# Attention with rotary positions and two feed-forward layers: loads of queries, keys, V and weights regrouped, one rotation on GpSimd alone, and the last products with V in two runs

## The chip, the cores and the metric

The kernel runs on one core of a Trainium2 chip. The metric is the device time of one execution in microseconds; less is better. TensorE (PE in the profile) multiplies matrices; its weight loads are shown as PEld. VectorE (DVE), ScalarE (ACT) and GpSimd (POOL) work on elements. SyncE (SP) issues the DMA transfers between HBM and on-chip memory. Each engine carries out its own instructions in order and waits for other engines by semaphores. TensorE's clock has two levels, 2.4 and 1.2 GHz; a granted clock of 1.00 is the upper one, 0.50 the lower.

## What is computed

The reference, cut to its core:

```python
def _attn_ref(q, k, v):            # (2, 8, 576, 64) each
    q_rot, k_rot = rotate(q), rotate(k)        # x1*cos - x2*sin, x1*sin + x2*cos
    scores = matmul(q_rot, k_rot^T) / sqrt(64)
    attn = exp(scores - max(scores))
    attn = attn / (sum(attn) + 1e-9)
    return matmul(attn, v)
def _moe_ref(x, w_in, w_out):      # 1152 tokens, 512 wide, 2048 hidden
    h = maximum(x @ w_in, 0)
    return h * h @ w_out
def _moe2_ref(x, w_a, w_b, w_out): # 512 wide, 1536 hidden
    return ((x @ w_a) * (x @ w_b)) @ w_out
```

Attention's output, heads side by side, is the input x of the first feed-forward layer, and that layer's output the input of the second.

## The kernel before

The sixteen heads are taken as eight pairs, p = 0 to 7; the two heads of a pair stand in the lower and upper 64 partitions. For each pair queries and keys are loaded into a tile X with planes for the value and for its half-swapped copy, each for queries and keys (`load_qk`, line 325); the load of a pair from 2 on is four transfers of 288 KB, one for each plane over all 128 partitions. `rotate` (line 344) multiplies by cosine and sine in place (line 356) and adds the two products (line 357), keys first, then queries. For pair 1 these four operations may go to VectorE or GpSimd; from pair 2 on GpSimd does them. X has two slots, so the load for pair p + 2 needs the rotation of pair p to be over.

A pair has five blocks c = 0 to 4, four of 128 query rows for each head and a fifth, half as much work, with the last 64 rows of both. For each block `scores` (line 383) puts eight matmuls (line 405, in the fifth block line 400) into one of two double banks `s0`, `s1`. VectorE takes them out with a negation that also finds the maximum (line 425), which frees the bank; ScalarE makes the exponentials and their sums (line 430); VectorE transposes them in blocks of 32 (line 446, `turned`). `times_v` (line 463) multiplies the transposed exponentials of the pair before with V, in five parts, into four banks AV[0] to AV[3], columns 0 to 192; one part is 64 or 48 small matmuls on TensorE (line 476). In TensorE's order, scores of the next block and a part of the products of the pair before alternate. Eight ScalarE copies (lines 307, 488 to 491) take the products out. `recip` (line 499) inverts the sums, with four small GpSimd operations (lines 509 to 512); `flip` (line 518) transposes them on TensorE, and `spread` (line 527) spreads them over partitions, into columns 192 to 480 of AV[0] and AV[1] for the last two pairs, where VectorE multiplies them with the products (line 542). Two more operations split the result into a high and a low part of x (lines 568 and 565).

`load_part` (line 452) runs after the blocks 0 to 3. It loads 32 partitions of V (288 KB, line 457) after a one-column ScalarE copy into the same place (line 455) that reads the sums of this block, so that the transfer can't start before the exponentials, and it hands in one of the four transfers of X of pair p + 2. That one is placed behind the copy in the plan, but does not touch what the copy writes.

Weights come as 64-bit words. `convert` (line 571) loads a raw tile of 512 KB (line 579, three slots), a ScalarE operation takes the upper halves (line 580), a clamp follows on GpSimd or VectorE (line 589), then a shift and a merge on VectorE (lines 583 and 586). The first `EARLY` = 4 weights are converted during attention: their clamp is on GpSimd, and the shift uses a score bank. The first three raw loads wait for a VectorE write into the slot (line 930) that follows the exponentials of the blocks named in `GATES`; conversions are spaced by `PACE` (line 906).

All operations are put into a `Plan` (line 69). TensorE's order is that in which they are written down. For the others the plan runs through time with a cost for each operation, gives every operation a due time worked back from TensorE, and takes the one that can start first, the earliest due among equals. A transfer costs 3.2 us for 1024 KB in the plan, plus 2.0 until others see it. The orders of TensorE, ScalarE, VectorE and GpSimd are then kept as planned (line 1001); SP is not in that list, and its order is made by the program builder from the data dependences.

After attention, `unit1` (line 690) makes a group of twelve matmuls of 384 columns for one block of the hidden layer, and `out1`, `super2` and `out2` do the rest of both layers, three matmuls for each product of numbers in two parts (lines 669 to 671, 876 to 878). The first list entries `steps` are unit1 for hidden blocks 0 to 3 with the first 384 tokens, which need only pairs 0 to 3; from the fifth entry on all pairs are needed. The loop at line 968 places what is left of the last two pairs between these entries at the places in `FILL`.

## Time and profile before

| | |
|---|---|
| median of 3 runs | 574.05 us (572.3 to 574.73) |
| the profiled execution | 578.77 us, of which its span, first to last instruction, is 577.0 us |
| TensorE busy | 550.0 us (95% of the span), 5318 matmuls |
| VectorE, GpSimd, ScalarE busy | 433.9, 305.3, 276.7 us |
| DMA | 58.45 MB, mean 101 GB/s |
| mean granted clock of TensorE | 0.967 |

The profile is one execution recorded on the chip. The table of stages gives for each stretch of time the busy time of each engine, with the number of instructions, the granted clock, the share of time that the DMA engines were busy, and their rate. The list of waits says which engine stood idle ahead of which line, and whose signal ended it ("issue" is idle time that ended without any signal that the profile shows). The chain of waits goes back in time from the last instruction, at each step to what released it. The timeline of an engine has start, duration, line, operation, output and input, count, and in brackets the idle time ahead of it with its releaser. The page's groups have busy time, mean nanoseconds of one, idle time ahead of them and its main releaser. The table of DMA issues has the number of transfers, their size, and the median time from issue to landing in us.

### The profile page before, as it was taken

Reading aid. Unit: us, or ns where it says so; the run is one execution under the profiler, and the core shown is the slowest. Engines: PE = TensorE matmul, PEld = TensorE weight load, DVE = VectorE, ACT = ScalarE, POOL = GpSimd, SP = SyncE. Lnnn points to the kernel's source line nnn. Section 1 sums busy time; section 2 is a strip of 40 time slices with the busy share of each in tenths; the row PEclk is TensorE's granted clock in tenths of the full one; section 3 lists DMA queues with packets and bytes.
Section 4 is the critical chain, followed back from the end, with each engine's and each line's share of the span. In section 5 each row is a group of like instructions: output and inputs, shape, how many; then the busy total and the mean of one; then the engine's idle time right before and its main releaser. Section 6 shows DMA issues by size and latency. Waiting matters only on the chain.

```text
span 577.0 us, 13042 instructions
## 1 busy us (share of the span) xinstructions
PE 550.0 (95%) x5318; PEld 491.5 (85%) x5318; DVE 433.9 (75%) x785; ACT 276.7 (48%) x652; POOL 305.3 (53%) x249
## 2 busy tenths in 40 slices
PE   7897689899889999999999999999999999999997
PEld 5565356666679999999999999999998999999986
DVE  5894697899639976944883759989787888886554
ACT  2453585667537756712730543565554544434210
POOL 2563798751327865812750537778676476765000
PEclk9798596899999999999999999999999999999999
DMA  7388377323204454411431201033331332310004
GB/s 239 112 224 209 121 232 191 91 74 84 65 3 154 157 202 145 147 36 37 149 108 37 73 1 37 2 110 132 123 101 51 108 110 74 110 38 1 1 0 164
DMA packets 18911, 58.45 MB, mean 101 GB/s; under 512 B 2313, under 2 KB 4489, under 8 KB 17828
## 3 DMA queue, kind: packets, MB, share of 16 engines
q1 hardware_dynamic: 18852, 57.63, 32.0%
q8 instruction: 41, 0.67, 0.5%
q14 instruction: 18, 0.15, 0.1%
HBM read 55.26 MB, written 2.36 MB: 100 GB/s over the span
## 4 chain that ended last, share of the span: by engine, by line
PE 83%; DVE 9%; DMA 3%; issue 2%; POOL 1%; ACT 1%; SPq 1%; DVEq 0%; ACTq 0%; POOLq 0%
PE m L669 13%; PE m L670 12%; PE m L671 12%; PE s L405 6%; PE av L476 6%; PE av L669 6%; PE av L670 6%; PE av L671 6%; PE m L876 3%; PE m L878 3%; PE m L877 3%; DMA raw_i<-in_w_in 2%; PE av L878 2%; PE av L877 2%; DMA X<-in_qk 2%
## 5 line engine op out<-in xcount | busy, mean ns | idle before, releaser
L565 POOL TENSOR_TENSOR g<-v,g 128x384 fp32r<-128x384 f32 (+1 forms) x41 | 48.9, 1195 | 43.0 <-ACT g L568 42.9
L430 ACT ACTIVATE PV<-PV,st 128x576 f32<-128x576 f32 x48 | 36.9, 769 | 40.5 <-DVE PV L425 40.3
L568 ACT CAST g<-v 128x384 fp32r<-128x384 f32 (+1 forms) x72 | 40.7, 566 | 25.9 <-DVE v L847 13.6
L425 DVE TENSOR_SCALAR_CACHE_REDUCE PV<-s 128x576 f32<-128x576 f32 x48 | 34.4, 753 | 11.9 <-PE s L405 11.6
L669 PE MATMUL m<-y,w_p 128*128 128x288 f32 x140 | 41.3, 295 | 0.7 <-DVE v L843 0.7
L670 PE MATMUL m<-y,w_p 128*128 128x288 f32 x140 | 41.2, 295 | 0.0
L671 PE MATMUL m<-y,w_p 128*128 128x288 f32 x140 | 41.1, 294 | 0.0
L405 PE MATMUL s<-cs_rot 64*128 64x288 f32 x128 | 32.0, 525 | 6.9 <-DVE PV L425 3.2
L476 PE MATMUL av<-PT_acc,PV 32*64 32x160 f32 (+1 forms) x1152 | 30.3, 326 | 7.2 <-issue 4.0
L356 POOL TENSOR_TENSOR X<-X,cs_rot 128x1152 f32<-128x1152 f32 x13 | 34.2, 2631 | 5.3 <-DMA X<-in_qk 5.3
L476 PEld LDWEIGHTS av<-PT_acc,PV 32*64 32x64 f32 x1152 | 23.5, 146 | 14.7 <-issue 9.2
L405 PEld LDWEIGHTS s<-cs_rot 64*128 64x128 f32 x128 | 17.6, 226 | 16.2 <-issue 6.8
L671 PE MATMUL m<-g,w_o 128*128 128x384 f32 (+1 forms) x92 | 29.3, 319 | 0.0
L670 PE MATMUL m<-g,w_o 128*128 128x384 f32 (+1 forms) x92 | 29.3, 318 | 0.0
L669 PE MATMUL m<-g,w_o 128*128 128x384 f32 (+1 forms) x92 | 29.3, 318 | 0.0
L708 DVE TENSOR_TENSOR v<-m,v 128x384 f32<-128x384 f32 x32 | 17.5, 551 | 15.3 <-ACT v L707 15.2
L589 POOL TENSOR_SCALAR cl_i<-cl_i 128x512 f32<-128x512 f32 x10 | 20.1, 2013 | 16.1 <-ACT cl_i L580 13.5
L717 DVE TENSOR_TENSOR oacc<-m,oacc 128x512 f32<-128x512 f32 (+1 forms) x29 | 19.4, 670 | 12.1 <-PE m L878 12.0
L669 PE MATMUL m<-x,w_i 128*128 128x384 f32 x84 | 28.5, 339 | 0.0
L717 DVE TENSOR_TENSOR yacc<-m,yacc 128x384 f32<-128x384 f32 (+1 forms) x28 | 14.2, 512 | 18.7 <-PE m L671 18.5
L671 PE MATMUL m<-x,w_i 128*128 128x384 f32 x84 | 28.1, 334 | 0.0
L670 PE MATMUL m<-x,w_i 128*128 128x384 f32 x84 | 28.1, 334 | 0.0
(246 smaller groups left out, 1958.2 us busy)
## 6 DMA issues: line engine op xcount, KB each, us to landing
PV<-in_vq SPq DMA_DIRECT2D x32, 288.0 KB, 3.4
raw_i<-in_w_in SPq DMA_DIRECT2D x16, 512.0 KB, 4.1
raw_o<-in_w_out SPq DMA_DIRECT2D x16, 512.0 KB, 3.7
X<-in_qk SPq DMA_DIRECT2D x26, 288.0 KB, 4.4
raw_a<-in_w_a SPq DMA_DIRECT2D x12, 512.0 KB, 3.7
raw_b<-in_w_b SPq DMA_DIRECT2D x12, 512.0 KB, 3.7
raw<-in_w_out SPq DMA_DIRECT2D x12, 512.0 KB, 3.6
out<-oacc SPq DMA_DIRECT2D x8, 256.0 KB, 2.0
```

The costliest lines, as they stand in the source:

```text
L356: m = pl.op(where, ("s", 2 * S), lambda e, qi=qi: e.tensor_tensor(out=x()[:, :, qi, :], in0=x()[:, :, qi, :], in1=cs, op=ALU.mult), [done[ ...
L405: pe.matmul(s[h]()[:, bk, 0:288], q0, k0[h][:, bk * 288:bk * 288 + 288], start=True, stop=True)
L425: m = pl.op("DVE", ("us", 0.7), lambda e, h=h, j=j: e.tensor_scalar(out=PP[pr.k][:, h, :].rearrange("p (b n) -> p b n", b=2), in0=s[h]()[: ...
L430: x = pl.op("ACT", ("us", 0.8), lambda e, h=h, j=j: e.activation(PP[pr.k][:, h, :], PP[pr.k][:, h, :], AF.Exp, bias=st()[:, 0, j:j + 1], s ...
L476: pe.matmul(AV[a]()[half(h), q], v[r, h, b], pt[r, k:k + 4 + both, 32 * b:32 * b + 32], start=(b == 0), stop=(b == KB - 1), skip_group_che ...
L565: e.tensor_tensor(out=out_, in0=a, in1=b, op=ALU.subtract)
L568: h = pl.op("ACT", ("s", n), lambda e: e.copy(hi_(), val()), after)
L669: pe.matmul(dst, wh, mh, start=first, stop=False, skip_group_check=open_)
L670: pe.matmul(dst, wh, ml, start=False, stop=False, skip_group_check=open_)
L671: pe.matmul(dst, wl, mh, start=False, stop=last, skip_group_check=open_)
L717: return pl.op("DVE", ("p", width), lambda e: e.tensor_tensor(out=acc(), in0=dst(), in1=acc(), op=ALU.add), [o] + b.prior, rel=[b])
L877: pe.matmul(b(), gt[:, 0, c], w[:, 1, d], start=False, stop=False)
```

## The change

Five things are edited.

- Queries and keys of pairs 2 to 7 are loaded in four parts of 32 partitions with all planes, after blocks 1 to 4 instead of one plane each after blocks 0 to 3. Behind blocks 3 and 4, where no part of V is loaded any more, a one-column ScalarE copy into the part of X comes first. `rotate` waits for all four parts.
- V's parts 0 and 1 are loaded after block 0, part 2 after block 1, part 3 after block 2 (`VAT`).
- The first three raw weight loads are gated by blocks (1,3), (2,0), (2,2) instead of (2,0), (2,2), (2,4), and in the plan every raw load ends `LATE` = 3.0 us later for those that wait for it.
- Pair 1 is rotated on GpSimd alone.
- Parts 0 and 1 of the last pair's products with V stay after the first entry of `steps`; parts 2 to 4 move behind the second one (`VFILL`). `flip` of the last pair, behind them, no longer waits in the plan for the products' banks.

```diff
+VAT = ((0, 1), (2,), (3,), (), ())
-GATES = ((2, 0), (2, 2), (2, 4))
+GATES = ((1, 3), (2, 0), (2, 2))
+VFILL = (0, 0, 1, 1, 1)
+LATE = 3.0
...
-            o.end, o.on, o.begin = s + took + self.LAG.get(e, 0.0), e, s
+            o.end, o.on, o.begin = s + took + o.late, e, s
...
-                for k, (qi, n) in enumerate(PLANES):
-                    LX[p, k] = lambda after, k=k, qi=qi, n=n: dma(288, lambda e: e.dma_start(out=b()[:, n, qi], in_=qk[p][:, n, qi]), after, acq=[] if k else [b])
+                for a in range(4):
+                    LX[p, a] = lambda after, a=a, r=slice(32 * a, 32 * a + 32): dma(288, lambda e: e.dma_start(out=b()[r], in_=qk[p][r]), after, acq=[] if a else [b])
...
-                where = FLEX if p == 1 else "POOL"
-                m = pl.op(where, ("s", 2 * S), lambda e, qi=qi: e.tensor_tensor(out=x()[:, :, qi, :], in0=x()[:, :, qi, :], in1=cs, op=ALU.mult), [done[qi, 0], done[qi, 1]])
+                where = "POOL"
+                m = pl.op(where, ("s", 2 * S), lambda e, qi=qi: e.tensor_tensor(out=x()[:, :, qi, :], in0=x()[:, :, qi, :], in1=cs, op=ALU.mult), list(done.values()))
...
-    def load_part(p, a):
-        r = slice(32 * a, 32 * a + 32)
-        ex, st = EXP[p, a][1][-1:], ST[p]
-        w = pl.op("ACT", ("us", 0.2), lambda e: e.copy(V4[r, p % 2, 0, 0, 0:1], st()[r, 1, 2 * a + 1:2 * a + 2]), ex + ([AVD[p - 2]] if p > 1 else []))
-        w.soon, w.anchor = 1.8, SDONE[p, a]
-        LV.setdefault(p, []).append(dma(288, lambda e: e.dma_start(out=V4[r, p % 2], in_=vq[p]), [w]))
-        if p + 2 < NPAIR:
-            if a == 0:
+    def load_part(p, c):
+        ex, st = EXP[p, c][1], ST[p]
+        for a in VAT[c]:
+            r = slice(32 * a, 32 * a + 32)
+            w = pl.op("ACT", ("us", 0.2), lambda e, r=r: e.copy(V4[r, p % 2, 0, 0, 0:1], st()[r, 1, 2 * c + 1:2 * c + 2]), ex[-1:] + ([AVD[p - 2]] if p > 1 else []))
+            w.soon, w.anchor = 1.8, SDONE[p, c]
+            LV.setdefault(p, []).append(dma(288, lambda e, r=r: e.dma_start(out=V4[r, p % 2], in_=vq[p]), [w]))
+        if c and p + 2 < NPAIR:
+            if c == 1:
                 load_qk_done[p + 2] = load_qk(p + 2)
-            load_qk_done[p + 2][PLANES[a]] = LX[p + 2, a]([w])
+            after = ex[-1:]
+            if not VAT[c]:
+                r = slice(32 * c - 32, 32 * c)
+                after = [pl.op("ACT", ("us", 0.2), lambda e: e.copy(XA[p + 2]()[r, 0, 0, 0:1], st()[r, 1, 2 * c:2 * c + 1]), ex[:1])]
+                after[0].soon, after[0].anchor = 1.8, SDONE[p, c]
+            load_qk_done[p + 2][c] = LX[p + 2, c - 1](after)
...
         o = pl.op("SP", ("dma", 512), lambda e: e.dma_start(out=raw_(), in_=src_of[key[0]][key[1]]), gate(), acq=[raw_])
+        o.late = LATE
...
-        if c < 4:
-            load_part(p, c)
+        load_part(p, c)
...
         if n == FILL[0]:
             last_spread(p - 1)
-            for k in range(len(PARTS)):
+        for k in range(len(PARTS)):
+            if n == VFILL[k]:
                 times_v(p, k)
         if n == FILL[1]:
-            flip(p, [Buf("av", None)], lambda: AV[2]().bitcast(BF16)[0:27, 896:1024])
+            flip(p, [], lambda: AV[2]().bitcast(BF16)[0:27, 896:1024])
```

## Rows read from the trace of the kernel before

**Rows 1.** Table of stages, cut where pairs 1 to 5 and unit1 begin.
```profile
27.34:41.10 13.76, 13.76 (x289) 9.30 (x288) 13.63 (x32) 8.54 (x24) 7.42 (x8) 1.00 0.72 189
41.10:68.18 27.08, 18.08 (x342) 11.73 (x339) 15.96 (x38) 11.65 (x37) 14.50 (x13) 0.76 0.71 181
68.18:86.00 17.82, 15.84 (x342) 10.76 (x339) 15.13 (x35) 11.75 (x36) 15.57 (x14) 0.88 0.71 220
86.00:106.15 20.15, 18.46 (x338) 12.32 (x338) 16.57 (x37) 12.71 (x38) 15.00 (x15) 0.75 0.69 180
106.15:120.67 14.52, 14.52 (x343) 10.13 (x338) 11.83 (x29) 9.93 (x31) 9.37 (x9) 0.88 0.26 75
...
168.76:577.00 408.24, 404.06 (x2505) 388.95 (x2502) 308.56 (x516) 186.93 (x375) 218.71 (x160) 1.00 0.25 85
```

**Rows 2.** List of waits of TensorE: waiting line, releaser, total us, times, longest.
```profile
PE s L400 <- DVE small L425: 6.6, 1, 6.6
...
PE s L405 <- DVE bits_i L586: 1.9, 2, 1.4
PE av L476 <- ACT PV L455: 1.4, 1, 1.4
```

**Rows 3.** Chain of waits, 46 to 60 us: start, duration, what.
```profile
46.09 1.42 POOL rot L357
...
47.53 0.33 SPq L330
...
49.80 10.05 DMA raw_i<-in_w_in
```

**Rows 4.** Timeline of ScalarE, the first weight's conversion.
```profile
59.88 0.66 ACT L580 ACTIVATE cl_i<-raw_i 128x512 f32<-128x512 f32 x1 [12.04 <-DMA raw_i<-in_w_in]
```

**Rows 5.** Timeline of VectorE in pair 0.
```profile
13.35 3.62 DVE L356 TENSOR_TENSOR X<-X,cs_rot 128x1152 f32<-128x1152 f32 x1
...
16.89 0.74 DVE L425 TENSOR_SCALAR_CACHE_REDUCE PV<-s 128x576 f32<-128x576 f32 x1
```

**Rows 6.** Timeline of TensorE, scores of pairs 0 and 1.
```profile
12.80 1.91 PE L405 MATMUL s<-cs_rot 64*128 64x288 f32 x8 [0.75 <-DVE PV L425]
...
17.79 2.87 PE L405 MATMUL s<-cs_rot 64*128 64x288 f32 x8 [2.21 <-DVE PV L425]
...
30.12 1.91 PE L405 MATMUL s<-rot 64*128 64x288 f32 x8
```

**Rows 7.** Timeline of GpSimd in pair 1, and the page's group of clamps.
```profile
31.38 2.64 POOL L356 TENSOR_TENSOR X<-X,cs_rot 128x1152 f32<-128x1152 f32 x1 [3.27 <-DMA X<-in_qk]
34.10 1.41 POOL L357 TENSOR_TENSOR cs_rot<-X 128x576 f32<-128x576 f32 x1
37.41 0.20 POOL L509 CAST part<-st 128x9 bf16<-128x9 f32 x1 [1.91 <-DVE st L506]
...
L589 POOL TENSOR_SCALAR cl_i<-cl_i 128x512 f32<-128x512 f32 x10 | 20.1, 2013 | 16.1 <-ACT cl_i L580 13.5
```

**Rows 8.** Timeline of ScalarE, exponentials of pair 0's last block.
```profile
28.00 0.77 ACT L430 ACTIVATE rot<-rot,st 128x576 f32<-128x576 f32 x1 [0.85 <-DVE rot L425]
```

**Rows 9.** DMA issues: X in 0:14, X in 27.3:41.1, V in 120.67:136.
```profile
X<-in_qk SPq DMA_DIRECT2D x4, 288.0 KB, 3.2
...
X<-in_qk SPq DMA_DIRECT2D x8, 288.0 KB, 5.3
...
PV<-in_vq SPq DMA_DIRECT2D x4, 288.0 KB, 3.2
```

**Rows 10.** Timeline of TensorE, the last pair's products with V.
```profile
155.11 3.02 PE L476 MATMUL av<-PT_acc,PV 32*64 32x160 f32 x138 [1.20 <-DVE xf L542]
159.43 2.42 PE L476 MATMUL av<-PT_acc,PV 32*64 32x160 f32 x128 [1.31 <-issue]
162.89 0.77 PE L476 MATMUL av<-PT_acc,PV 32*64 32x160 f32 x22 [1.03 <-issue]
```

**Rows 11.** Timeline of ScalarE, the copies that take these products out.
```profile
163.53 1.19 ACT L307 COPY xf<-av 128x128 f32<-128x128 f32 x8 [7.59 <-PE av L476]
```

More of the change, by code (lines that the diff above doesn't have):

```diff
@@ L62, in __init__ @@
         self.deps, self.acq, self.rel = list(deps), list(acq), list(rel)
-        self.end, self.soon, self.anchor, self.slack, self.urgent = None, None, None, 0.0, False
+        self.end, self.soon, self.anchor, self.slack, self.urgent, self.late = None, None, None, 0.0, False, 0.0
     def after(self, deps):
@@ L72 @@
     HOP = {"PE": 0.25, "SP": 2.0, "-": 0.0}
-    LAG = {}
     PORT = {"DVE": "POOL", "POOL": "DVE"}
@@ L322, in attention_moe_moe2_kernel @@
     XA, LX = {}, {}
-    PLANES = ((1, 0), (1, 1), (0, 0), (0, 1))
     def load_qk(p):
```

## The prediction

> **What bounds the kernel now.** I read the stage table first. Each pair of heads is cut where its first scores start, so that one line is one pair. From 168.76 us on, TensorE is busy for 404.06 of 408.24 us at full clock: nothing in this diff takes a matmul away there, so that part is fixed. Before it, the pairs take very unequal times for nearly equal work: 13.76, 27.08, 17.82, 20.15 and 14.52 us [rows 1]. With pair 5 as the measure, pair 2 has 12.6 us too many, pair 4 5.6 and pair 3 3.3, and the clock of these three is 0.75 to 0.88. Pair 0 fills the 27.34 us ahead of pair 1.
>
> Next the list of what TensorE waited for. The longest entry by far is one wait of 6.6 us for VectorE, in pair 2 [rows 2]. To see who made VectorE late, follow the chain of waits back through that place: GpSimd's last rotation of pair 3 ends at 47.51, only then does SP issue (47.53) the next of four loads of queries and keys, and the first weight tile goes out behind them at 49.80 and lands 10.05 us later [rows 3]. ScalarE meanwhile stands for 12.04 us at the conversion that wants this tile, with the exponentials behind it in its queue [rows 4]. SP is not among the engines whose order the plan writes out (line 1001), and counted from the start, four for a pair, these loads are those of pair 5, two pairs ahead.
>
> **The change, part by part.** The sum is made against the profiled execution, 578.77 us with a span of 577.0 (1.77 around it). It lies 4.7 us above the median of the three runs, 574.05.
>
> *GpSimd alone rotates pair 1.* In the kernel before, VectorE did one multiplication of 3.62 us at 13.35, and its next negation (`L425`), which frees a score bank, came at 16.89 [rows 5]. TensorE therefore idled for 2.21 us, and the following scores ran at half clock: 2.87 us for eight matmuls, where the same eight take 1.91 at full clock at 30.12 [rows 6]. Without that multiplication the first negation can begin when the second scores end, about 14.7 (they start at 12.80 and take 1.9). One negation of 0.7 us later there is a bank, so the third scores start at 15.4 instead of 17.79: 2.4 us. From there to pair 1 went 27.34 - 17.79 = 9.55 us; at full clock two steps of 2.78 (30.12 less pair 1's start at 27.34) and the short fifth block, for which I estimate 2.1 from these, give 7.7. Together -4.2 us; bounds -2.4 (the clock falls anyway) and -4.5. GpSimd must now do both products and sums, 2 x (2.64 + 1.41) = 8.1 us [rows 7], from about 13.2 to 21.3; pair 1 would start at 23.2, so 1.9 us hide it.
>
> *Rotation after the fourth part.* Until now the keys were rotated when their two planes had landed. Now the first multiplication waits for all four parts, and the fourth is tied by a ScalarE copy to the exponentials of the pair's last block. For pair 2 that block's exponential starts at 28.00 and takes 0.77 [rows 8]; the copy and the issue add about 0.5, the landing 3.2 to 5.3 us [rows 9], of which I take 4.2, near the middle, since V's and X's loads of one block still overlap; then 8.1 us on GpSimd, and the four small operations of line 509 on (1.1 us with their gaps) [rows 7], which fall into the middle and keep the flip in TensorE's queue waiting too. 28.8 + 0.5 + 4.2 + 8.1 + 1.1 = 42.7, where pair 2 started at 41.10: a new wait. All of it moves with pair 0's gain, so the price is +1.6 us, bounds 0.5 (landing 3.2) and +3 (landing 5.3, and the flip's delay on top). Behind it stand the scores and everything after them on TensorE. For pairs 3 to 7 the last exponential comes before or just at the next pair's start, so rotation ends some 13 us into a pair of 14.5 to 17: hidden, with 1.5 us to spare. Clamps of the early weights (two per pair in pairs 2 and 3) share GpSimd, so I add +0.5 for all five, bounds -0.5 and +5.
>
> *V sooner, first weights sooner, loads in parts.* V's last part is loaded after the third block, not the fourth; the 1.4 us wait on it (released through `L455`) [rows 2] goes. The first weight is gated on block (1,3) instead of (2,0), two blocks or about 5 us earlier, while its conversion stays paced by (2,0). Two of the four loads of a pair can't run ahead now, because a ScalarE copy writes into their tile first; the other two can, but only when the old rotation is done, which is now near the same pair's start. So the four loads of pair 5 no longer stand before the weight, and `LATE` puts the conversion later in ScalarE's order. Each conversion still costs VectorE 1.3 us by the plan's own figure (line 593) and may hold a score bank (1.9 us over two waits in pairs 2 to 4, [rows 2]). Pair 2 thus becomes like pair 3, which has two conversions: 17.82, less 1.3 for its share of half clock (0.12 x 17.82 = 2.1 us at most, part of which VectorE hides), 16.5. That is -10.6 us; bounds 14.5 (pair 5) and 24 (raw tile still half as late), so -12.5 and -3. Pair 3 itself: -1.3, bounds -3 and +1. Pair 4 ran at 0.75; I give it the middle between itself and pair 5, 17.3, which is -2.9, bounds -5 and 0. ScalarE's two extra copies of 0.2 us a pair lie in its idle time.
>
> A part now covers 32 partitions with rows four times as long. The rows show no penalty: undisturbed, V's loads, which have this very form, land in 3.2 us and the 128-partition planes of X also in 3.2 [rows 9]. The Trainium skill (SBUF — State Buffer, "Door 1: The DMA port swizzle") says otherwise: 32 partitions reach 8 of 16 ports, about 218 GB/s instead of 436. By that page a 288 KB part takes some 0.7 us longer on the wire, an estimate from its two rates; with three such parts queued the last one would be 2 us later, and the wait at pair 2 would be 3.6 instead of 1.6 us. The trace does not bear it out for single loads; for queued ones no row shows it.
>
> *Last pair's products in two runs.* Before, 288 products ran in one piece and TensorE stopped twice with nothing to wait for, 1.31 and 1.03 us, 128 products apart [rows 10]: it looks as if the stream of instructions ran dry. From one stop's end to the next is 162.89 - 159.43 = 3.5 us, the time that a stretch of 128 then takes to arrive. In the new order the 128 of the first two parts are followed by twelve large matmuls (2.3 us), then 160. The first stretch takes about 118 x 0.019 (2.42 / 128) plus ten of the twelve large ones, 1.9, so 4.1 us, and its stop goes; the second about 3.0 us, and keeps 0.5 of 1.03. That is -1.8. But the flip now follows the products at once. It writes into bank AV[2], which eight ScalarE copies of 1.19 us in all read [rows 11]. The same trace shows TensorE waiting 1.20 us for a VectorE operation that only reads other columns of its bank [rows 10], so I charge +1.0. Net -0.8, bounds -2.3 and +1.2. The flip has no cover: it stands in TensorE's queue ahead of unit1's third group, so a wait twice as long costs 1.0 more.
>
> *`LATE` on all weights* changes only the order of conversions after 168.76, where TensorE is 99% busy: 0, bounds -1 and +3.
>
> Sum: -4.2 + 1.6 + 0.5 - 10.6 - 1.3 - 2.9 - 0.8 = **-17.7 us**. Against the profiled execution that is 561.1; against the median 556.4. Part of the 4.7 us between these may be just the half-clock stretches that the change shortens, so I take a value between the two, nearer to the median's, **558 us**; its own range is 552 to 565.
>
> **The rivals.**
> *First weight still late.* SP's order is not in the plan, and two parts of each pair may still slip ahead and wait there for GpSimd. For: that is what happened at 41 to 47.5 [rows 3]. Against: two of four are now tied, and the gate is 5 us earlier. Then pair 2 keeps 7 to 9 us of its stall; 566 us. This is also the case in which the change doesn't do what it says.
> *GpSimd's rotation becomes the bound (slower).* Every pair from 2 on starts only when its rotation ends. A landing of 7.6 us instead of 4.2 under load (between X's 5.3 and the weight's 10.05 [rows 3, 9]), plus two clamps of 2.01 us ahead [rows 7], make 0.5 + 7.6 + 8.1 + 4.0 = 20.2 us per pair against 14.5: +5.7 in six pairs, 34 us, less the 17.7 gained, is 16 above the median: 590. It decides for slower from about 3.5 us per pair (six times that is 21, the gain and 0.5% of the time together). For: GpSimd was already busy for 15.57 of 17.82 us in pair 3 [rows 1]. Against: clamps have no early due time, and in pairs 5 to 7 there are none. At half that price, 17 us less 17.7, nothing would be left of the gain but a few us: 571 to 574.
> *The loads in parts land later.* Queued parts of 32 partitions may be slower than single ones; then the last part is late at pair 2, by up to the distance between the landings of 3.2 and 5.3 us [rows 9], 2 us: 560. For: in pairs 1 to 3 all loads queue. Against: V's loads in this form. By the port rule of that page of the Trainium skill this case would be the rule.
>
> **How the numbers follow.** Forecast 0.66; first weight late 0.12; the parts landing later 0.08; GpSimd at half price 0.06, at full price 0.08. The time is that of the likeliest. 551 to 568 takes in the forecast with the lower ends of its terms, the late weight and the late parts, and leaves out GpSimd's cases. About 0.5% is what a measurement of this kernel can tell from no change. Faster by more than that is everything up to 571: 0.66 + 0.12 + 0.08 and a sixth of the half-price case, 0.87; the rest of that case, 0.05, is no change, and the full price, 0.08, is slower.
>
> **What would show it.** In the changed kernel: the scores after 14.64 start near 15.4, with no multiplication at line 356 on VectorE; ScalarE's wait for the first weight falls from 12 us to under 2; TensorE's 6.6 us entry is gone and pair 2 takes under 18 us; a new wait of 0 to 3 us on GpSimd's rotation stands ahead of pair 2; the two stops in the last products shrink to one, with a wait on ScalarE's copies at the flip. From the fourth matmul group of unit1 on, the rest lasts 408 us as before. The prediction is wrong if the weight's load again leaves after loads of a later pair, or if rotation waits stand ahead of every pair.

## The result and the profile after

The changed kernel takes **565.52 us** (median of 4 runs, 563.62 to 566.12); the kernel before took 573.17 us in the runs beside it. The ratio is 0.9863, 95% interval 0.9821 to 0.9905: 7.65 us or 1.4% faster. The forecast was 558, its range 551 to 568: the direction and the range hold, the gain is about half of the 16 us that were forecast against the median. The profiled execution took 565.88 us with a span of 563.8, where before it was 578.77 and 577.0. Between the two spans the difference is 13.2 us, and why that is more than 7.65 is the first thing to be explained. The profiled execution of the kernel before counts as a slow one; e1 below profiles that kernel again.

The stage table of the changed kernel, cut as [rows 1] (pairs 1 to 5, then the rest from unit1's fourth group of matmuls on): the stretch, its length, busy time and instructions of TensorE, its weight loads, VectorE, ScalarE and GpSimd, then granted clock, DMA share and GB/s.

```profile
22.57:37.04 14.47, 14.20 (x289) 9.26 (x288) 13.42 (x32) 8.65 (x25) 8.76 (x8) 1.00 0.66 166
37.04:55.68 18.64, 15.13 (x341) 9.71 (x339) 15.83 (x37) 12.70 (x40) 12.07 (x11) 0.97 0.86 201
55.68:75.22 19.54, 17.97 (x340) 11.83 (x339) 14.77 (x35) 12.29 (x38) 15.06 (x13) 0.77 0.77 201
75.22:94.50 19.28, 17.19 (x338) 11.59 (x338) 17.64 (x34) 12.28 (x37) 14.57 (x13) 0.82 0.66 173
94.50:110.35 15.85, 14.73 (x344) 9.63 (x339) 13.76 (x32) 11.18 (x37) 10.26 (x10) 1.00 0.63 154
155.80:563.80 408.00, 403.90 (x2505) 388.90 (x2502) 311.96 (x517) 187.21 (x375) 213.32 (x159) 1.00 0.26 85
```

Pair 2 fell from 27.08 to 18.64 us, and pair 1 begins at 22.57 instead of 27.34. But pair 3 is longer than before (19.54 after 17.82), pair 4 hardly shorter (19.28 after 20.15), pair 5 longer (15.85 after 14.52), and pairs 3 and 4 run at granted clocks of 0.77 and 0.82. The last stretch is the 408 us that were expected.

What TensorE waited for, over the whole span (waiting line, releaser, total us, times, longest):

```profile
PE r L528 <- DVE bits_i L594: 2.5, 1, 2.5
PE s L406 <- DVE PV L426: 2.3, 6, 0.6
PE s L406 <- issue: 1.5, 2, 0.9
PE av L483 <- DVE xf L549: 1.2, 1, 1.2
PE s L406 <- DVE bits_i L594: 1.1, 2, 0.6
```

The entry of 6.6 us [rows 2] is gone, and so is the wait for V's last part. The longest left is 2.5 us, at a flip, for the bits of a weight.

Why the 6.6 us went is seen in SP's queue. First the kernel before, then the changed one, then ScalarE's conversion of the first weight in the changed one (a row of SP's timeline joins neighbours of a kind: start, time from the first issue to the end of the last, line, tile, count):

```profile
40.84 8.45 SPq L330 DMA_DIRECT2D X<-in_qk  x6
49.39 0.37 SPq L457 DMA_DIRECT2D PV<-in_vq  x1
49.80 0.42 SPq L579 DMA_DIRECT2D raw_i<-in_w_in  x1
50.33 14.64 SPq L457 DMA_DIRECT2D PV<-in_vq  x3
65.07 0.85 SPq L579 DMA_DIRECT2D raw_i<-in_w_in  x2
```

```profile
36.56 0.31 SPq L331 DMA_DIRECT2D X<-in_qk  x1
36.93 0.66 SPq L586 DMA_DIRECT2D raw_i<-in_w_in  x1
38.18 0.31 SPq L331 DMA_DIRECT2D X<-in_qk  x1
...
44.48 0.38 SPq L586 DMA_DIRECT2D raw_i<-in_w_in  x1
...
61.05 0.85 SPq L586 DMA_DIRECT2D raw_i<-in_w_in  x2
...
44.85 0.67 ACT L588 ACTIVATE cl_i<-raw_i 128x512 f32<-128x512 f32 x1
```

Before, six loads of X stood ahead of the first weight and held the queue for 8.45 us; after, the weight leaves at 36.93 with single loads of X around it, and ScalarE's conversion has no wait beside it, where it had 12.04 us [rows 4].

The tail, answering to [rows 10] (TensorE), with ScalarE's copies, answering to [rows 11]:

```profile
144.63 2.99 PE L483 MATMUL av<-PT_acc,PV 32*64 32x160 f32 x128 [1.20 <-DVE xf L549]
...
149.83 3.17 PE L483 MATMUL av<-PT_acc,PV 32*64 32x160 f32 x160
152.93 0.23 PE L528 MATMUL av<-small,part 128*27 128x128 bf16 x1
...
152.87 1.20 ACT L309 COPY xf<-av 128x128 f32<-128x128 f32 x8 [0.95 <-PE av L483]
```

Both stops within the products are gone, and the flip at 152.93 starts with no wait just after the first of ScalarE's copies of the products began at 152.87.

### The profile page after: what moved, and what is told of

Read it like the earlier page. It is cut to its first block, busy times and chain, and to the rows that moved or that the text cites. A ratio compares the mean times of both kernels' runs of the same rounds, so it can differ in the third digit from the quotient of the medians.

```text
span 563.8 us, 13068 instructions
## 1 busy us (share of the span) xinstructions
PE 547.1 (97%) x5318; PEld 488.6 (87%) x5318; DVE 435.6 (77%) x785; ACT 280.2 (50%) x664; POOL 302.2 (54%) x249
## 4 chain that ended last, share of the span: by engine, by line
PE 82%; DVE 9%; ACT 3%; DMA 2%; issue 2%; POOL 1%; SPq 0%; DVEq 0%; ACTq 0%; POOLq 0%
PE m L677 13%; PE m L679 13%; PE m L678 13%; PE av L677 6%; PE av L678 6%; PE av L679 6%; PE av L483 6%; PE s L406 4%; PE m L886 3%; PE m L885 3%; PE m L884 3%; DMA X<-in_qk 2%; DVE PV L426 1%; PE av L886 1%; PE av L885 1%
## 5 line engine op out<-in xcount | busy, mean ns | idle before, releaser
L572 POOL TENSOR_TENSOR g<-v,g 128x384 fp32r<-128x384 f32 (+1 forms) x39 | 47.4, 1217 | 47.0 <-ACT g L575 46.7
L575 ACT CAST g<-v 128x384 fp32r<-128x384 f32 (+1 forms) x72 | 40.8, 567 | 30.8 <-DVE v L855 16.2
L678 PE MATMUL m<-y,w_p 128*128 128x288 f32 x152 | 44.8, 295 | 0.0
L679 PE MATMUL m<-y,w_p 128*128 128x288 f32 x152 | 44.7, 294 | 0.0
L677 PE MATMUL m<-y,w_p 128*128 128x288 f32 x152 | 44.7, 294 | 0.0
L357 POOL TENSOR_TENSOR X<-X,cs_rot 128x1152 f32<-128x1152 f32 x14 | 36.6, 2634 | 11.4 <-DMA X<-in_qk 8.5
L406 PE MATMUL s<-cs_rot 64*128 64x288 f32 x128 | 28.4, 455 | 4.7 <-DVE PV L426 2.0
L406 PE MATMUL s<-rot 64*128 64x288 f32 x128 | 29.6, 473 | 1.3 <-issue 0.9
L483 PE MATMUL av<-PT_acc,PV 32*64 32x160 f32 (+1 forms) x1152 | 29.0, 315 | 1.6 <-DVE xf L549 1.2
L725 DVE TENSOR_TENSOR oacc<-m,oacc 128x512 f32<-128x512 f32 (+1 forms) x32 | 21.6, 679 | 10.9 <-PE m L886 10.8
L678 PEld LDWEIGHTS m<-y,w_p 128*128 128x128 f32 x152 | 28.5, 188 | 1.0
L677 PEld LDWEIGHTS m<-y,w_p 128*128 128x128 f32 x152 | 28.5, 188 | 0.9
L716 DVE TENSOR_TENSOR v<-m,v 128x384 f32<-128x384 f32 x32 | 17.6, 552 | 15.0 <-ACT v L715 15.0
L572 POOL TENSOR_TENSOR w_i<-bits_i,w_i 128x512 fp32r<-128x512 f32 x10 | 13.0, 1302 | 29.4 <-ACT w_i L575 29.3
L572 DVE TENSOR_TENSOR g<-v,g 128x384 fp32r<-128x384 f32 (+1 forms) x33 | 24.2, 732 | 5.8 <-ACT g L575 5.6
L679 PEld LDWEIGHTS m<-y,w_p 128*128 128x128 f32 x152 | 28.6, 188 | 0.0
```

The source lines that it names most:

```text
L357: m = pl.op(where, ("s", 2 * S), lambda e, qi=qi: e.tensor_tensor(out=x()[:, :, qi, :], in0=x()[:, :, qi, :], in1=cs, op=ALU.mult), list(d ...
L406: pe.matmul(s[h]()[:, bk, 0:288], q0, k0[h][:, bk * 288:bk * 288 + 288], start=True, stop=True)
L483: pe.matmul(AV[a]()[half(h), q], v[r, h, b], pt[r, k:k + 4 + both, 32 * b:32 * b + 32], start=(b == 0), stop=(b == KB - 1), skip_group_che ...
L572: e.tensor_tensor(out=out_, in0=a, in1=b, op=ALU.subtract)
L575: h = pl.op("ACT", ("s", n), lambda e: e.copy(hi_(), val()), after)
L677: pe.matmul(dst, wh, mh, start=first, stop=False, skip_group_check=open_)
```

## The experiments

The table gives, for each kernel, its median and its ratio to the kernel before (with interval) and, from its profiled execution, the start of pair 1, the lengths of pairs 1 to 5, and the time from pair 7's start to the end. The kernel before had medians of 571.9 to 573.6 us in the runs beside e1 to e12.

| kernel | median us | ratio (95%) | pair 1 at | pairs 1 / 2 / 3 / 4 / 5 | pair 7 to end |
|---|---|---|---|---|---|
| before | 574.05 | – | 27.34 | 13.76 / 27.08 / 17.82 / 20.15 / 14.52 | 441.1 |
| changed | 565.52 | 0.9863 (0.9821–0.9905) | 22.57 | 14.47 / 18.64 / 19.54 / 19.28 / 15.85 | 438.7 |
| e1_before_again | 572.83 | 1.0021 (0.9988–1.0054) | 22.97 | 13.78 / 28.56 / 17.25 / 19.20 / 15.12 | 441.2 |
| e2_pool1_alone | 572.43 | 1.0003 (0.9979–1.0028) | 23.65 | 14.46 / 23.38 / 17.72 / 19.62 / 15.03 | 441.0 |
| e3_gates_undone | 569.33 | 0.9955 (0.9939–0.9971) | 23.52 | 14.46 / 20.34 / 21.08 / 16.73 / 17.64 | 440.2 |
| e4_clamp_vector | 570.26 | 0.9963 (0.9930–0.9997) | 23.83 | 14.47 / 18.85 / 20.43 / 18.89 / 17.98 | 440.2 |
| e5_split_undone | 565.84 | 0.9871 (0.9819–0.9923) | 23.35 | 14.46 / 18.30 / 19.98 / 17.27 / 15.84 | 441.5 |
| e6_loads_undone | 571.16 | 0.9962 (0.9937–0.9987) | 23.12 | 14.46 / 19.86 / 16.17 / 23.84 / 14.47 | 441.5 |
| e7_shift_in_sbuf | 568.74 | 0.9928 (0.9903–0.9953) | 23.14 | 14.46 / 18.16 / 16.58 / 21.91 / 16.24 | 440.2 |
| e8_no_small_add | 566.54 | 0.9882 (0.9833–0.9931) | 23.80 | 14.46 / 17.81 / 17.70 / 20.21 / 17.98 | 440.3 |
| e9_bridge | 566.99 | 0.9910 (0.9876–0.9944) | 23.75 | 14.46 / 20.14 / 17.30 / 19.15 / 14.65 | 440.2 |
| e10_v_undone | 564.56 | 0.9857 (0.9804–0.9910) | 24.10 | 14.46 / 17.15 / 20.01 / 18.21 / 15.48 | 438.8 |
| e11_late0 | 566.42 | 0.9882 (0.9822–0.9942) | 23.07 | 14.46 / 16.15 / 19.83 / 18.37 / 18.65 | 439.8 |
| e12_two_alone | 563.37 | 0.9835 (0.9790–0.9881) | 23.18 | 15.42 / 15.43 / 21.03 / 15.58 / 15.26 | 440.9 |

### Was the profiled execution of before typical?

The kernel before, unchanged, profiled once more; and the kernel before with one line of the change.

> The kernel before, unchanged, profiled once more. The first profiled execution took 578.77 us, 5.6 more than the median 573.17. Theory: that execution was an unlucky one, and the extra time lies in the stretches at half clock of pairs 2 to 4 (65.05 us in all); this profile then shows a span of about 571 with some 60 us for the three pairs, and the wait of ScalarE for the first weight still over 8 us. Rival: the profile itself adds the time; then the span is 576 to 577 again, with the three pairs at 65.

```
-                where = FLEX if p == 1 else "POOL"
+                where = "POOL"
```

> The kernel before with pair 1 rotated on GpSimd alone, nothing else. Theory: pair 1 starts at about 22.6 instead of 27.3 us, as in the changed kernel, and all that follows moves with it, since the load that the first weight waited behind hangs on the same rotations: 568.5 to 569.5 (-4). Rival: the wait in pair 2 is set by loads that don't move and eats it: 572 to 573.

e2 took the rival's 572.4 us. Neither theory foresaw what e1 showed: pair 1 began at 22.97 with no line changed, while pairs 2 to 4 took the same 65.0 us as in the first profile. The profiled execution of e1 took 575.89 us, still 3.1 above its median, so it isn't a typical one either. That of e2, whose edit turned out to be worth nothing, took 571.86, within 0.6 us of its median; its pair 2 took 23.38 us, with a wait of 5.73 us for the first weight where the two others had 12.04 and 13.53. The rows are those of the one multiplication on VectorE. First GpSimd in the first profile of before (VectorE's row beside it is in [rows 5]), then VectorE and GpSimd in e1:

```profile
13.12 2.63 POOL L356 TENSOR_TENSOR X<-X,cs_rot 128x1152 f32<-128x1152 f32 x1 [1.20 <-DMA X<-in_qk]
```

```profile
13.22 1.35 DVE L356 TENSOR_TENSOR X<-X,cs_rot 128x1152 f32<-128x1152 f32 x1
...
13.47 3.59 POOL L356 TENSOR_TENSOR X<-X,cs_rot 128x1152 f32<-128x1152 f32 x1 [1.68 <-DMA X<-in_qk]
```

In the first profile GpSimd began 0.23 us ahead of VectorE, and VectorE's operation took 3.62 us; in e1 VectorE began 0.25 us ahead and took 1.35, and GpSimd's took 3.59 instead of 2.63. So the 3.62 us on which the first term of the sum rested hung on which of two operations started a quarter of a microsecond ahead of the other. Taken alone, in e2, the line is worth nothing: 1.0003, with pair 1 longer by 0.7 us.

### The parts undone, one at a time

```
-GATES = ((1, 3), (2, 0), (2, 2))
+GATES = ((2, 0), (2, 2), (2, 4))
```

> The changed kernel with the first three raw weights gated as before, by blocks (2,0), (2,2), (2,4). Theory: what had made the first weight late were the loads of a later pair in front of it, and the tied loads in parts cure that alone; the load then leaves some 5 us later and lands about when the conversion wants it: 565 to 567, ScalarE waits under 3 us. Rival: the earlier gate is the cure; then ScalarE waits 4 us or more for the weight and the time is 568 to 571.

```
-                for a in range(4):
-                    LX[p, a] = lambda after, a=a, r=slice(32 * a, 32 * a + 32): dma(288, lambda e: e.dma_start(out=b()[r], in_=qk[p][r]), after, acq=[] if a else [b])
+                for k, (qi, n) in enumerate(PLANES):
+                    LX[p, k] = lambda after, k=k, qi=qi, n=n: dma(288, lambda e: e.dma_start(out=b()[:, n, qi], in_=qk[p][:, n, qi]), after, acq=[] if k else [b])
```

> The changed kernel with one part undone: X loaded by planes (keys first, two planes, then queries) instead of by 32 partitions, V's parts one after each of the first four score groups as before, and the rotation of keys waits for its own two planes alone. Gates, split, pair 1 and the later due time of the weights stay as changed. Theory: the rotation that waits for all four parts is what holds GpSimd's clamp back in pair 2 (a wait of 2.83 us for X, with the clamp behind it at 49.59 us); with planes the rotation of keys starts earlier, the clamp and the shift behind it come earlier, and the time falls to 562 to 564.5 us beside 565.5. Rival: V's earlier parts and the loads by partitions are worth as much as they cost or more, and planes bring back longer waits for V or for queries: 566.5 to 569.5 us.

Both cost: 3.8 us against the changed kernel for the gates (569.33, the rival's time, but without the wait of ScalarE that the rival named) and 5.6 us for the loads (571.16, beyond even the rival's). SP's queue and ScalarE in e3, then in e6:

```profile
43.13 0.41 SPq L586 DMA_DIRECT2D raw_i<-in_w_in  x1
...
51.73 0.66 ACT L588 ACTIVATE cl_i<-raw_i 128x512 f32<-128x512 f32 x1
```

```profile
37.48 0.42 SPq L581 DMA_DIRECT2D raw_i<-in_w_in  x1
37.95 7.58 SPq L332 DMA_DIRECT2D X<-in_qk  x4
...
62.58 1.75 SPq L332 DMA_DIRECT2D X<-in_qk  x4
...
64.90 0.85 SPq L581 DMA_DIRECT2D raw_i<-in_w_in  x2
...
73.34 0.66 ACT L583 ACTIVATE cl_i<-raw_i 128x512 f32<-128x512 f32 x1 [3.77 <-DMA raw_i<-in_w_in]
```

(The diff of the loads is cut to the transfers of X; the blocks behind which they leave, V's place and the rotation's waits are as before there too.) With the old gates the first weight leaves at 43.13 instead of 36.93 and its conversion comes at 51.73 instead of 44.85; pair 3 then takes 21.08 us. In this trace TensorE also stops for 3.40 us, with no signal that ends it, near the end of pair 2 (until 57.59); whether that belongs to the gates is not shown. With the old loads the first weight leaves in time (37.48), but four planes of X hold the queue for 7.58 us right behind it, and later four more stand ahead of the third weight. It leaves at 64.90 (61.05 in the changed kernel), ScalarE waits 3.77 us for it, and its conversion comes at 73.34, where pair 4 begins; that pair takes 23.84 us. So the two parts do different things for the same weights: the gates let the first one leave early, and the loads in parts keep the later ones from standing behind loads of X that are not wanted yet. Each without the other leaves a gain of 0.4%, the two together 1.4% or more (e12 below).

The other parts, undone:

```
-VFILL = (0, 0, 1, 1, 1)
+VFILL = (0, 0, 0, 0, 0)
...
-            flip(p, [], lambda: AV[2]().bitcast(BF16)[0:27, 896:1024])
+            flip(p, [Buf("av", None)], lambda: AV[2]().bitcast(BF16)[0:27, 896:1024])
```

> The changed kernel with one part undone: the last pair's five groups of products with V are issued in one run again, behind the first unit, and the transpose of the sums' parts acquires the banks again. In the changed kernel the stretch from the first product of the MoE's first unit to the end of the last group took 15.14 us, where it took 17.62 us in the kernel before. Theory: the whole 2.5 us belongs to the split, so this kernel takes 567.5 to 568.5 us beside the changed kernel's 565.5, and the two stops of TensorE in the fourth and fifth groups are back, between 1 and 2 us each. Rival: only the 0.8 us of the prediction belong to the split, the rest being the earlier arrival of what the last pair needs; then 566 to 566.8 us.

```
-VAT = ((0, 1), (2,), (3,), (), ())
+VAT = ((0,), (1,), (2,), (3,), ())
```

> The changed kernel with V's parts loaded after the first four score groups, one each, as before; X stays in parts of 32 partitions after groups two to five, and all else as changed. With planes for X and the old place of V together the time was 571.16 us beside the changed kernel's 565.5, with waits of TensorE for V (1.7 us) and for products of the pair before the last (2.8 us). Theory: V's late last part, which lies behind X's plane in the queue, makes that loss: 568.5 to 571 us here too. Rival: the form and order of X's loads makes it, V's place does not matter: 565 to 567 us.

```
-LATE = 3.0
+LATE = 0.0
```

> The changed kernel with the estimate of the weights' landing 3 us shorter, as before. The order that the planner writes changes: ScalarE converts the first early weight ahead of the exponentials of its group instead of behind the first of them, and the same for the third and fourth. Theory: the weights land by then (ScalarE did not wait for the first at 44.85 us), so the place is worth less than 1 us: 565 to 567 us. Rival: the conversion moves ahead of the landing, ScalarE waits for the raw weight in pair 2 with exponentials queued behind it, and pair 2 takes over 20 us: 568 to 571 us.

None of the three moves the time by what these runs can tell from nothing (+0.3, -1.0 and +0.9 us against 565.52, each with intervals of about 3 us to either side). So it was not V's place that cost 5.6 us in e6, but the form and order of X's loads. With `LATE` at 0 the first conversion does not wait either (the second waits 1.15 us; pair 2 took 16.15 us), against its rival. Without the split the stops within the last products come back: one of 1.24 us in e5, two of 0.89 and 1.31 in e12 below. The split is small, and the last column of the table gives its size best: from pair 7's start to the end the nine traces with the split take 438.7 to 441.5 us, 440.0 in the mean, and the five without it 440.9 to 441.5, 441.1 in the mean. That is 1.1 us, between groups that overlap and that differ in other parts too, nearer to the 0.8 of the forecast than to the 2.5 that the first pair of profiles seemed to show.

### Where the rest of the gain went

Four theories about the stops that are left in pairs 2 to 5. In the changed kernel the longest begins as follows (GpSimd, VectorE, TensorE):

```profile
44.40 5.23 POOL L357 TENSOR_TENSOR X<-X,cs_rot 128x1152 f32<-128x1152 f32 x2 [2.83 <-DMA X<-in_qk]
49.59 1.92 POOL L597 TENSOR_SCALAR cl_i<-cl_i 128x512 f32<-128x512 f32 x1
...
51.55 0.69 DVE L591 TENSOR_SCALAR up_i<-cl_i 128x512 int32<-128x512 int32 x1 [1.31 <-POOL cl_i L597]
52.28 0.69 DVE L594 SCALAR_TENSOR_TENSOR bits_i<-raw_i,up_i 128x512 int32<-128x512 int32 x1
...
53.11 0.22 PE L528 MATMUL r<-small,part 128*27 128x128 bf16 x1 [2.52 <-DVE bits_i L594]
```

ScalarE has converted the weight by 45.5, but the clamp stands on GpSimd behind the rotation of pair 3, which waits 2.83 us for X's fourth part. VectorE waits for the clamp, the flip waits for a score bank that the shift's result holds, and from 54.5 us on the granted clock is at its lower level (0.50) for 10.2 us.

The clamps on VectorE:

```
-            o = pl.op("POOL", ("clamp", DM), lambda e: clamp(e, cl), [o])
-            o = pl.op("DVE", ("us", 1.3), lambda e: (shift(e, cl), merge(e)), [o], acq=[up] + bits.acq, rel=[raw_, cl, up])
+            o = pl.op("DVE", ("us", 2.0), lambda e: (clamp(e, up), shift(e, up), merge(e)), [o], acq=[up] + bits.acq, rel=[raw_, cl, up])
```

> The changed kernel with the clamps of the first four weights on VectorE, into the score bank that the shift uses anyway, instead of on GpSimd. Theory: in the changed kernel the first clamp stood behind pair 3's rotation on GpSimd (49.59, though its input was ready at 45.5), VectorE stood 1.31 us for it, TensorE 2.52 us, and the clock then fell to half for 10.24 us; with the clamp off GpSimd that wait and this stretch go: 560 to 562. Rival: it is the shift's hold of a score bank that stops TensorE, and this makes it 0.7 us longer: 565 to 568.

The time rose by 4.7 us, and the waits for bits of a weight grew from 3.6 us (2.5 and 1.1 in the list above) to 6.5:

```profile
PE s L406 <- DVE bits_i L594: 4.7, 3, 2.1
...
PE r L528 <- DVE bits_i L594: 1.8, 1, 1.8
```

So moving the clamp to VectorE costs more than it gives. What its place on GpSimd costs by itself is not shown, since the edit also makes VectorE hold the bank longer. The bank itself is tried with this edit, after which shift and merge hold none (with `up` taken out of the list of what is acquired and released):

```
-        up = Buf(STAGS, {t: lazy(lambda t=t: sps.tile([P, 2, 512], F32, tag=t, name=f"up_{name}")[:, 0]) for t in STAGS}) if early else bank_t()
+        up = cl if early else bank_t()
```

> The changed kernel in which the four early conversions shift in place in the clamped tile in SBUF, and merge from there, so that they hold no bank of the scores. Theory: TensorE's longest remaining waits (2.5 and 1.1 us for bits of a weight) and the half clock behind them come from the score bank that shift and merge hold while the shift waits for GpSimd's clamp; without the bank pair 2 to pair 5 lose 3 to 5 us together (73.3 us now, 68 to 70 then), 560.5 to 562.5 us, and no wait of TensorE for bits of a weight is left in the attention. Rival: the shift, now with both ends in SBUF, is stretched by GpSimd's products (from 0.69 to 2 us or more), VectorE's negations wait behind it, and the waits only change their name: 565 to 569 us.

The waits for bits are gone, as meant, and the time is 3.2 us worse. The price is on VectorE, where shift and merge now read and write SBUF (two of the four weights):

```profile
51.55 1.59 DVE L591 TENSOR_SCALAR cl_i<-cl_i 128x512 int32<-128x512 int32 x1
53.17 1.77 DVE L594 SCALAR_TENSOR_TENSOR bits_i<-raw_i,cl_i 128x512 int32<-128x512 int32 x1
...
81.53 0.89 DVE L591 TENSOR_SCALAR cl_i<-cl_i 128x512 int32<-128x512 int32 x1
82.46 3.00 DVE L594 SCALAR_TENSOR_TENSOR bits_i<-raw_i,cl_i 128x512 int32<-128x512 int32 x1
```

0.69 us became up to 3.00 beside GpSimd's products, and TensorE's longest wait for VectorE's negations (line 426) rose from 0.6 to 2.2 us: the rival's mechanism. So e7 doesn't show what the bank costs by itself. Then the small addition, which in the changed kernel took this long:

```profile
81.11 2.55 DVE L512 TENSOR_SCALAR st<-st 128x9 f32<-128x9 f32 x1
...
81.00 5.21 POOL L357 TENSOR_TENSOR X<-X,cs_rot 128x1152 f32<-128x1152 f32 x2 [3.47 <-DMA X<-in_qk]
```

```
-            e.tensor_scalar_add(st()[:, 1, :], st()[:, 1, :], 1e-9)
+            pass
```

> The changed kernel without the addition of 1e-9 to the sums of exponentials (128 by 9 elements, once in each pair), which took 2.55 us beside GpSimd's product in pair 3, 0.13 to 0.17 us elsewhere. This addition is left out of the computation. Theory: this 2.55 us stood ahead of the negation of scores on VectorE, TensorE waited for it and fell to the half clock at 81.8 us; without it pair 3 takes 16 to 17.5 us instead of 19.28, and the kernel 562 to 563.5 us. Rival: the wait for GpSimd passes to VectorE's next operation between SBUF and SBUF (reciprocal or transposition), or the stop in pair 3 has another cause: 565 to 566 us.

566.54: no gain, as the rival had it. In that trace TensorE's longest wait is a flip's, 2.4 us for GpSimd's parts of the sums, in pair 4. The fourth, idle products of TensorE across the stop:

```
+BRIDGE = {(2, 4): 12}
...
+        if (p, c) in BRIDGE:
+            pl.op("PE", ("us", 0.0), lambda e: [pe.matmul(AV[3]()[:, 480:512], ZERO, ZERO[:, 0:32], start=True, stop=True, skip_group_check=True) for k in range(BRIDGE[p, c])], [o])
```

> The changed kernel with 12 idle products of TensorE (zeros by zeros, 32 columns, into columns of a bank that nothing reads) between the last scores and the transpose of the sums' parts in pair 2, where TensorE stood still for 2.52 us (50.6 to 53.1) and the granted clock fell from 54.5 us on. Theory: the half clock is what the forecast of pairs 3 and 4 left out (TensorE is busy for 17.97 us in pair 3, for 14.7 in pair 5 at full clock with the same work); without the stop the clock stays at 1.00 in pair 3, pair 3 takes 16 to 17.5 us instead of 19.54, and the time is 562 to 564 us. Rival: in pair 3 GpSimd (15.06 us busy) and VectorE (14.77) are the limit, TensorE's slower products only fill its waits; the clock stays up and pair 3 takes 18.5 us or more, 565 to 566.5 us.

(These products open a new accumulation in that bank, so they change what pair 1's products with V leave there; what is issued otherwise stays the same.) Pairs 2 to 4 of that kernel, then VectorE's merge of the first weight, the last scores of pair 2 and the idle products:

```profile
38.22:58.36 20.14, 18.57 (x365) 13.17 (x363) 15.38 (x37) 12.21 (x38) 13.83 (x11) 0.92 0.75 187
58.36:75.66 17.30, 15.34 (x342) 10.60 (x339) 16.29 (x35) 12.67 (x40) 13.40 (x12) 0.90 0.78 207
75.66:94.81 19.15, 18.64 (x338) 12.18 (x338) 15.28 (x34) 12.43 (x37) 13.76 (x13) 0.73 0.78 192
...
53.10 0.69 DVE L597 SCALAR_TENSOR_TENSOR bits_i<-raw_i,up_i 128x512 int32<-128x512 int32 x1
...
52.83 1.21 PE L402 MATMUL s<-cs_rot 64*64 64x288 f32 x8
53.96 2.87 PE L425 MATMUL av<-small 128*128 128x32 f32 x24
```

Pair 3 became 2.2 us shorter at a clock of 0.90, but pair 2 longer by 1.5, and pair 4 ran at 0.73: 566.99 (10 runs), nothing gained: neither theory's time, though pair 3 came out as the first said. But in this execution the stop that was to be bridged was not there. The merge that the flip would have waited for ended at 53.79 (53.10 + 0.69), before the last scores (52.83 + 1.21 = 54.04), so that the 2.87 us of idle products came on top. e9 therefore doesn't decide between the two theories.

### The two parts that are left, alone

Against the kernel before, cut to the constants and the transfers of X:

```
+VAT = ((0,), (1,), (2,), (3,), ())
-GATES = ((2, 0), (2, 2), (2, 4))
+GATES = ((1, 3), (2, 0), (2, 2))
...
-                    LX[p, k] = lambda after, k=k, qi=qi, n=n: dma(288, lambda e: e.dma_start(out=b()[:, n, qi], in_=qk[p][:, n, qi]), after, acq=[] if k else [b])
+                    LX[p, a] = lambda after, a=a, r=slice(32 * a, 32 * a + 32): dma(288, lambda e: e.dma_start(out=b()[r], in_=qk[p][r]), after, acq=[] if a else [b])
```

> The kernel before with two parts of the change alone: X in parts of 32 partitions, loaded after groups two to five, and the gates of the weights one step earlier. Pair 1's rotation, V's place, the weights' due time and the run of the last products are as before. Theory: undoing either of these two took away 4 to 6 us of the changed kernel's gain and undoing any of the others nothing, so the two together are the whole gain: 564 to 567 us, pair 2 below 19 us. Rival: the other parts are each worth a microsecond that the single runs were too wide to show (V and the split above all); then this kernel takes 568 to 570 us.

563.37 us, 0.9835 of the kernel before: the whole gain, and the lowest median of all kernels here, though its interval overlaps the changed kernel's, so that the 2.1 us between them are not shown. Its pairs 2 to 4:

```profile
38.60:54.03 15.43, 14.01 (x342) 9.83 (x339) 13.85 (x35) 11.24 (x35) 12.29 (x10) 1.00 0.87 226
54.03:75.06 21.03, 17.58 (x341) 11.91 (x339) 17.32 (x37) 12.59 (x41) 14.85 (x14) 0.84 0.74 194
75.06:90.65 15.59, 14.36 (x339) 9.76 (x339) 14.86 (x34) 11.57 (x35) 14.61 (x13) 1.00 0.81 209
```

## Why the prediction was right or wrong

*What bounds the kernel, and pair 2 (right).* The reading of [rows 2] to [rows 4], a weight that leaves late behind loads of X, is what the change removed; e3, e6 and e12 show that gates and loads are the gain. Pair 2 was forecast at 16.5 us, or under 18, and took 18.64, with a new stop of 2.52 us in it. That is 8.4 us less than in the first profile, where the term was 10.6, and 9.9 less than in e1 (28.56). But both of those executions lay above their medians (by 4.7 and 3.1 us); against e2 (23.38), which lay close to its own, it is 4.7 less. So a part of the 10.6 belonged to the profiled execution, as all of the next term did. In e12 pair 2 took 15.43. The conversion's wait fell from 12.04 us to none, against "under 2".

*Pair 0 (wrong).* The term of -4.2 us failed, not in its mechanism but in what it was measured against. The multiplication of 3.62 us on VectorE [rows 5] did delay the scores, and without it they started at 14.42 in the changed kernel (15.4 forecast); the scores before them had already started at 11.20 there, where the forecast took 12.80, so from one to the next it was 3.22 us and not 2.6. But in e1 the same multiplication took 1.35 us, pair 1 began at 22.97, and in e2 the edit was worth 0. The term belongs to one profiled execution. The 4.7 us by which that execution lay above its median are of this size (27.34 - 22.97 = 4.4), though e1 lay 3.1 above its own with pair 1 at 22.97, so that this start alone need not be the gap. The prediction saw the gap and gave it to half-clock stretches, then took a value between the two; it should have left this term out of the sum against the median. That makes -13.5 against 574.05, 560.5 us.

*The rotation after the fourth part (wrong).* No wait for GpSimd's rotation stands ahead of pair 2 or any other pair, where +1.6 us was charged. GpSimd in pair 1 of the changed kernel:

```profile
27.44 5.24 POOL L357 TENSOR_TENSOR X<-X,cs_rot 128x1152 f32<-128x1152 f32 x2
32.62 2.79 POOL L358 TENSOR_TENSOR cs_rot<-X 128x576 f32<-128x576 f32 x2
```

The rotation of pair 2 ended at 35.41, 1.6 us ahead of that pair's scores at 37.04. The four small operations, charged 1.1 us in the middle of it, ran ahead of it (26.42 to 27.46), and then GpSimd had no wait for the fourth part. Pair 1 is longer by 0.7 us (14.47 after 13.78 in e1), but it is so in e2 as well, with the old loads, so that this goes with the rotation of pair 1 on GpSimd alone. The wait for the fourth part shows up elsewhere: on GpSimd, 2.83 and 3.47 us, with a clamp behind it in the first case. What it costs there is not isolated.

*Pairs 3 and 4 (wrong).* These are the larger part of what is missing. Forecast were 1.3 and 2.9 us less; against e1 pair 3 is 2.3 us longer and pair 4 0.1 longer, 38.8 us together where 33.8 were expected. The step that failed is that both were costed as if the half clock left them together with the stall in pair 2. It did not: the clock was 0.77 and 0.82. How such pairs compare, the traces of all kernels tell: pair 3 or 4 took 17.2 us in the mean of the four cases with a granted clock of 1.00 (15.6 to 18.4; e5, e8, e11, e12), and 20.3 us in the mean of the fifteen with 0.73 to 0.84 (18.9 to 23.8), pairs 3 and 4 of the changed kernel among them. In the nine cases between, with 0.87 to 0.96, it took 17.6 us (16.2 to 20.2), hardly more than at 1.00. So only long stretches at the lower level go with long pairs, and since the stops lie in the same pairs, the 3 us between the groups are not the price of the clock alone. In the changed kernel TensorE is busy for 17.97 and 17.19 us in them, against 14.73 in pair 5 at full clock for the same products: 5.7 us of longer matmuls, beside 5.0 us missing. That the stops cause the lower clock is what their order suggests (it fell 1.4 us after the stop of 2.52 ended); it is not shown. What sets off the low stretch stays open: none of the four edits shortened the whole, and only e8 takes a supposed cause away and adds nothing; in e8 the low stretches moved and the time stayed. e4 and e7 brought a cost of their own on VectorE, and e9 didn't meet its stop, so that these three don't rule their causes out. TensorE, VectorE and GpSimd are each busy for 14.6 to 18.0 of their 19 us there, so a delay on any of them is passed on; that this is why the stops only wander is argued, not shown.

*The last products in two runs (right in size, in part by luck).* -0.8 was forecast; 1.1 us in the mean over fourteen traces. But two steps in it were wrong: the second stretch's stop was to keep 0.5 us and kept none, and the +1.0 us for the flip behind ScalarE's copies did not appear (152.93, the copies begun at 152.87). Without these two charges the sum would have been -2.3, so the saving of the stops was put too high by about as much. Of the eight copies only two read the flip's bank AV[2], not all of them.

*`LATE` (right).* 0 was forecast; e11 is +0.9, within its interval, and the last stretch took 408.00 us.

*The rivals.* The first weight did not stay late; e3 and e6 show what each half of the change alone would have left, 569 and 571 us, where the rival said 566. GpSimd's rotation did not become the bound: TensorE has no wait on it at the start of any pair, and GpSimd's own waits for X's parts were 3.47 us at most. Loads in parts: between 22 and 80 us X's parts land in 5.9 us (median), V's in 5.1, where X's planes took 5.3 and V 3.5 in the kernel before and 5.1 and 4.1 in e1. That is 0.6 to 0.8 us later for X. By the port rule of the Trainium skill ("SBUF — State Buffer", "Door 1: The DMA port swizzle") the estimate was 0.7 us for a part; these medians lie there, but they don't show that rule at work. V's loads, of the same form in both kernels, land 1.0 to 1.6 us later too, and in e12, with X in parts, X takes 5.0 us, no more than e1's planes. So no run here shows a price of the form. Undoing it cost 5.6 us.

## What to carry to other kernels

Before a term is taken from one profiled execution, ask whether it hangs on two starts that lie within a fraction of a microsecond of each other, and whether the gap between that execution and the median is of its size; if so, profile the kernel again before it is counted as a gain of the change. Where a stall ends in a DMA, read the issuing queue for what stands ahead of it: here two parts of six (V's place and `LATE` counted by themselves), both about when things leave in that queue, were the whole gain. And when a long stall goes, do not let the clock of its neighbours go with it in the sum: cost them at the clock that they have until something shows that it rises.

## What the runs showed of the hardware

*VectorE and GpSimd.* The same two multiplications took 3.62 and 2.63 us with GpSimd first, 1.35 and 3.59 with VectorE first; the one that came second finished about when the first one's time and its own had both passed (13.12 + 2.63 + 1.35 = 17.10, and it ended at 16.97). The addition of 128 by 9 elements took 2.55 us beside GpSimd's product begun 0.11 us earlier (it ended at 83.66, and half of the two products at 83.6). The Trainium skill ("SBUF — State Buffer", "Who interferes with whom") has it that the one that issues first keeps the shared pair for the whole instruction, and that the order of issue decides who blocks; these rows agree. What was not expected is how little decides: with one of the two ahead by a quarter of a microsecond, or the other, pair 1 started 4.4 us apart in two executions of one kernel.

*Small matmuls in one run.* The last pair's 288 products in one run stop twice, in the kernel before for 1.31 and 1.03 us [rows 10]. With twelve large matmuls between the first 128 and the rest, 160 of them ran in 3.17 us with no stop. That the stream of instructions runs dry there, as the prediction has it, fits these rows; no run tests it.

*Reading beside writing (not shown).* TensorE's flip wrote into a bank at 152.93, for 0.23 us, while ScalarE's copies of four banks, begun at 152.87, were under way. But the copies of 128 columns start 0.16 us apart, and that of the flip's bank AV[2] is the third as the kernel writes them, from 153.20 on, so that the flip was over by then. The trace doesn't tell whether a read and a write of one bank would have got in each other's way. The 1.20 us wait of [rows 10] was taken as the price of such a place; it stands in the changed kernel too (144.63), and is one that the kernel orders itself: `last_spread` gives the banks back only when its operations on VectorE end, while the flip now acquires nothing.
